# State products from rounded values and remainders, first weight tile ahead of x, and eight plans instead of four

## The chip, the cores and the metric

One core of one Trainium2 chip. The time is device microseconds of one execution. A profiled execution adds a trace of every instruction of the engines: PE (TensorE matmul), PEld (its weight loads), DVE (VectorE), ACT (ScalarE), POOL (GpSimd) and SP (SyncE, which here only issues DMAs).

## What is computed

Eight batches of 512 tokens `x` and 32 state rows `state`, eight heads of 64. Tokens read from the state and the state reads from the tokens, by softmax attention; both results go through a feed-forward layer with a squared ReLU.

```python
scale = 1.0 / np.sqrt(D)
a = softmax(scale * x @ state.T)         # per batch and head; 1e-9 in the denominator
xread = a @ state
a2 = softmax(scale * state @ x.T)
sread = a2 @ x
rows = concatenate([xread, sread])       # 8 * (512 + 32) = 4608 rows of 512
h = rows @ w_in                          # 512 x 2048
r = np.maximum(h, 0.0)
out = (r * r) @ w_out                    # 2048 x 512
```

The host only changes layouts, and hands `w_in` and `w_out` over as the two 32-bit words of float64 numbers, which the kernel turns into float32 itself.

## The kernel before, in words

**Algebra.** `xread` is never formed. Since `(a @ state) @ w_in = a @ (state @ w_in)`, the kernel makes `z = state @ w_in` for each head and uses it as the weight of the product with `a`.

**Two kinds of products.** A float32 matmul shows as two records in the trace. Most products are instead written as three matmuls on a rounded value (`hi`, type fp32r) and the remainder (`lo`): hi·hi, lo·hi, hi·lo. `split` (line 333) makes the two: a cast on ACT, then a subtraction on DVE or POOL.

**Units.** Work goes batch by batch (0 to 7) and within a batch over 16 blocks of 128 columns of `w_in` (`fc`); one (batch, block) pair is a unit. In a unit `up` (line 718) makes `h` in PSUM tile `ph` from `a_hi`, `a_lo` and `z_hi`, `z_lo` (six matmuls of 512 columns), then ReLU on ACT, the square on DVE or ACT, and the split into `g_hi` and `g_lo`. `down` (line 750) adds 12 matmuls of 512 columns into the four PSUM tiles `po`. After the last batch, 16 narrower units (256 columns) treat the state's rows.

**State products.** `z_part(G, k, g)` (line 401) makes `z` for four batches at a time (G 0: batches 0 to 3, G 1: batches 4 to 7), for a pair of blocks `k` and half of the heads `g`: 16 calls for each G. Each call has four float32 matmuls of 256 columns (line 410). Each of them uses 64 of the array's 128 rows; the two halves (`own`) alternate. Two ACT copies bring the result from PSUM to `z_stage`, and a DMA brings that to memory (`zd`). `z_fetch` (line 454) reads back what one batch needs, in four DMAs, and splits it. For the first six blocks of batch 0, `z_direct` (line 433) makes `z` without memory. The 16 calls for G 1 are put in when the code comes to batch 2.

**The start.** `w_tile(fc)` loads a 512 KB tile of `w_in` and `singles` (line 345) turns it into float32: an ACT step (line 352) and three DVE steps (lines 356, 361, 367). `wo_tile` does the same for `w_out` and splits the result. All of these tiles share four buffers with the tag `raw`. `scores(0, g)` loads `x` in two halves and makes the attention weights of batch 0, in a chain that goes between PE, ACT and DVE (`sq`, line 517, is its first product). `pad(0)` loads the state into the zeroed tile `sp_f`. Until there is something to do, PE works on up to 40 filler groups of four small matmuls (`keep_busy`, line 785, tile `idle`), at 0.4 us each in the plan.

**Who sets the order.** Every step is an `op` with an engine (or a choice of engines), a modelled cost, and the buffers that it reads and writes. `Planner.plan` (line 135) gives each op a due time, going back from the units' own due times (`plan.when`, line 328) by modelled costs and by `slack` times a scale. It then simulates the engines and takes, of the ops that can begin first, the one due first. A load counts its size / 330 + 2.2 us in the model. `Planner.run` (line 205) makes one plan for each of four scales, takes the one that ends first in the model, and issues the instructions in that order; on the chip each engine goes through its list in order and waits by semaphores.

Of the kernel before, what the change touches and what calls it, by code (L numbers as in the profile page):

```python
# [9 lines left out]
F32 = mybir.dt.float32  # L10
F32R = mybir.dt.float32r
# [33 lines left out]
class Planner:  # L45
# [1 line left out]

    RATE = 330.0
    NEAR = 1.0
    SLACKS = (1.5, 2.0, 2.5, 3.0)  # L50

    def __init__(self):
        self.ops, self.last_w, self.readers, self.chains = [], {}, {}, {}
        self.when = []

    def op(
        self, engs, run, r=(), w=(), lat=0.2, due=1e9, begin=0.0, size=0, both=False, hold=None,
# [147 lines left out]
    def run(self):  # L205

        plans = []
        for scale in self.SLACKS:
            log = self.plan(scale)
            plans.append((max(o.end for _, _, _, o in log), scale, log))  # L210
        log = min(plans)[2]
        for _, _, e, o in log:
            for k in o.bufs:
                if k.t is None:
                    k.t = k.make()
            o.run(e)
        return log
# [10 lines left out]
def dve(n):  # L228
    return ("DVE", 0.07 + n / 960)
# [6 lines left out]
def gps(n):  # L236
    return ("POOL", 0.15 + n / 450)
# [3 lines left out]
def memory_attention_then_relu2_ffn(  # L241
# [10 lines left out]
    nc = tc.nc  # L252
    P = 128
    B, C, S = xT.shape
    D = stT.shape[0]
    H = C // D
    N = stT.shape[1] // (H * B)
    DM, DF = w_out.shape[1] // 2, w_out.shape[0]
    R = S + N
    NG = H * N // P  # L260
    HG = H // NG
    NCC = DM // P
    NQ = NCC // NG
    NFC = DF // P
    NT = S // P
    FW = 256
    NFCH = DF // FW
    FPC = FW // P
    GB = P // N
# [9 lines left out]
    PLAIN_X = 2  # L279
    WARM = 40  # L280
    PARTS = [(b, 0, NFC) for b in range(B)]
    START, FIRST, STEP = 14.0, 4.9, 4.4

    const = ctx.enter_context(tc.tile_pool(name="const", bufs=1))
    sb = ctx.enter_context(tc.tile_pool(name="sb", bufs=2))
# [6 lines left out]
        raw=4, xraw=2, x_hl=1, z_stage=2, st_z=1, z_raw=2, z_hi=2, z_lo=2, a_hi=2, a_lo=2,  # L292
        sp_raw=2, st=2, at=1, st_low=1, q1=2, e2=4, s2=4, nm2=2, m1=2, s1=2, e_hl=1, both=1, low=1,
        r=2, g_hi=2, g_lo=2, os_=3, wof=2, po=4, ph=2, px=2,
    )

    plan = Planner()
    op = plan.op

    def tile_(shape, dtype, name, tag=None):  # L300
        tag = tag or name
        pool = {"po": ps_o, "ph": ps_h, "px": ps_x}.get(tag, sb)
        return Buf(pool, shape, dtype, name, tag, BUFS[tag], hot=tag in ("px", "x_hl"))
# [3 lines left out]
    sp_hl = const.tile([P, NG, 2, 2, 2 * N], F32R, name="sp_hl")  # L307
    sp_f = const.tile([P, NG, 2, P + D], F32, name="sp_f")
    nc.vector.memset(sp_f, 0.0)
    warm = const.tile([P, P], mybir.dt.bfloat16, name="warm")  # L310
    nc.vector.memset(warm, 0.0)
    nc.gpsimd.memset(sp_hl.bitcast(F32), 0.0)
    sr = [const.tile([P, C], F32, name=f"sr{i}") for i in range(NGB)]
    wi = const.tile([P, NFC, NCC, P], F32, name="wi")
    wo = [
# [8 lines left out]
    units = [(b, fc) for b, lo, hi in PARTS for fc in range(lo, hi)]  # L324
    begins = {}
    for u, (b, fc) in enumerate(units):
        begins.setdefault(b, u)
    plan.when = [START + FIRST * min(u, NFC) + STEP * max(0, u - NFC) for u in range(len(units))]
    plan.when += [plan.when[-1] + STEP + 2.8 * fc for fc in range(NFC + 1)]

    ENGINE = {"DVE": nc.vector, "POOL": nc.gpsimd, "SP": nc.sync, "ACT": nc.scalar}

    def split(hi, lo, src, n, r, wh, wl, engs=None, due=1e9, both=True, chain=None):

        op(
            act(n, 0.03 if both else 0.0), lambda e: nc.scalar.copy(out=hi(), in_=src()),  # L336
            r=r, w=wh, due=due, chain=chain,
        )
        op(
            engs or [dve(n)],  # L340
            lambda e: ENGINE[e].tensor_sub(out=lo(), in0=src(), in1=hi().bitcast(F32)),  # L341
            r=[*r, *wh], w=wl, due=due, both=both,
        )
# [29 lines left out]
    def load(out, in_, size, r=(), w=(), due=1e9, begin=0.0, hold=30.0, issue=0.42, eng="SP", chain=None, land=2.2):  # L373
        op(
            (eng, issue), lambda e: ENGINE[e].dma_start(out=out(), in_=in_()),
            r=r, w=w, size=size, due=due, begin=begin, hold=hold, chain=chain, land=land, slack=2.0,
        )


    def w_tile(fc):  # L380
        raw = tile_([P, NCC, P, 2], I32, "w_raw", "raw")
        load(lambda: raw.t.rearrange("p c f w -> p (c f w)"), lambda: w_in[fc], 512, w=[raw])
        singles(lambda: wi[:, fc], lambda: raw.t, [raw], [("wi", fc)])

    st = {}

    def z_state(G):
# [10 lines left out]
        half(1)  # L398
        st[G] = raw

    def z_part(G, k, g, begin=0.0):
        pz = [tile_([P, NQ, FW], F32, f"pz{i}", "px") for i in range(2)]
        stage = tile_([P, NQ, 2, FW], F32, "z_stage")

        def product(e):
            for q in range(NQ):
                for i in range(2):
                    own = slice(i * D, (i + 1) * D)
                    cc = g * NQ + q
                    nc.tensor.matmul(  # L410
                        pz[i].t[:, q, :], lhsT=st[G].t[own, cc, :], rhs=wi[own, k * FPC:(k + 1) * FPC, cc, :],
                        start=True, stop=True,
                    )

        op(("PE", 1.2), product, r=[("wi", k * FPC + i) for i in range(FPC)] + [(st[G], 0), (st[G], 1)], w=pz, begin=begin)
        for i in range(2):
            op(
                act(512), lambda e, i=i: nc.scalar.copy(out=stage.t[:, :, i, :], in_=pz[i].t),  # L418
                r=[pz[i]], w=[(stage, i)],
            )  # L420
        load(
            lambda: zd[G, k][:, g].rearrange("p h f -> p (h f)"),
            lambda: stage.t.rearrange("p q i f -> p (q i f)"), 512,
            r=[(stage, 0), (stage, 1)], w=[("zd", G, k, g)], eng="ACT", issue=0.35, hold=None, land=4.5,
        )
# [46 lines left out]
    def pad(b):  # L472
        pairs[b] = [tile_([P, NG, S], F32R, n) for n in ("a_hi", "a_lo")]
        src = stP[b].rearrange("p (g q n) -> p g q n", g=NG, q=2)
        rows = [slice(i * D, (i + 1) * D) for i in range(2)]
        at = [slice(i * N, (i + 1) * N) for i in range(2)]
        if b == 0:
            for i in range(2):
                load(
                    lambda i=i: sp_f[rows[i], :, :, at[i]], lambda i=i: src[rows[i]], 32,  # L480
                    w=[f"sp_f{i}"], issue=0.6, due=-4.0 - i,
                )
            return
        raw = tile_([P, NG, 2, N], F32, "sp_raw")
        load(lambda: raw.t, lambda: src, 64, w=[raw])
        for i in range(2):
            if b < PLAIN_X:
                op(
                    dve2(2 * N * NG), lambda e, i=i: nc.vector.tensor_copy(
                        out=sp_f[rows[i], :, :, at[i]], in_=raw.t[rows[i]]),  # L490
                    r=[raw], w=[f"sp_f{i}"],
                )
                continue
            split(
                lambda i=i: sp_hl[rows[i], :, :, 0, at[i]], lambda i=i: sp_hl[rows[i], :, :, 1, at[i]],
                lambda i=i: raw.t[rows[i]], 2 * N * NG, [raw], [("sp_hi", i)], [("sp_lo", i)],
            )
# [4 lines left out]
    def scores(b, g):  # L502
        xt = tile_([P, NQ, S], F32, "xt_raw", "xraw")
        load(
            lambda: xt.t, lambda: xT[b, g * CG:(g + 1) * CG, :].rearrange("(q p) s -> p q s", p=P),
            512, w=[xt], chain="x", due=1e9 if b else -10.0 + 8 * g,
        )
        q1 = tile_([P, NJ, N], F32, "q1")
        nm2 = tile_([P, 1], F32, "nm2")
# [15 lines left out]
        else:  # L525
            pst = tile_([P, S], F32, "st")
            for q in range(NQ):
# [8 lines left out]
                def product(e, hl=hl, pq=pq, q=q):  # L536
# [9 lines left out]
                    w=[pq],  # L546
# [292 lines left out]
    u = 0  # L839
    for b, lo, hi in PARTS:  # L840
        if b not in started:
            pad(b)
            for g in range(NG):
                scores(b, g)
            started.add(b)
        if lo == 0 and b >= 1:
            for g in range(NG):
                read(b - 1, g, At(begins[b] + 8), At(begins[b] - 1))
        if b == 2 and not z1[0]:
            z1[0] = True  # L850
            z_state(1)
            for m in range(NFC):
                z_part(1, *divmod(m, NG), begin=At(begins[2] + m * (begins[GB] - begins[2]) / (NFC + 4) - 1))
        po = [tile_([P, DM], F32, f"po{t}", "po") for t in range(NT)]
        for fc in range(lo, hi):
            k, i = divmod(fc, FPC)
            if (b, k) not in zs or (fc == lo and lo):
                z_fetch(b, k)
            f = slice(i * P, (i + 1) * P)

            z_hi, z_lo = zs[b, k]

            def todo(z_hi=z_hi, z_lo=z_lo, b=b, f=f):
                a_hi, a_lo = pairs[b]
                return [
                    (w.t[:, g, f], v.t[:, g, :])
                    for w, v in ((z_hi, a_hi), (z_lo, a_hi), (z_hi, a_lo))
                    for g in range(NG)
                ]

            r = [(z_hi, i), (z_lo, i)] + [(a, g) for a in pairs[b] for g in range(NG)]
            g_ = up(fc, S, todo, r, 3 * NG * pe(S)[1], u)
            down(po, fc, g_, fc == lo, fc == hi - 1, At(u + 2, -1.0))
            u += 1
        finish_part(b, lo, hi, po, At(u + 1))
    read(B - 1, 0, At(u - 6))
# [86 lines left out]
```

## Time and profile before

| | us |
|---|---|
| median of 3 runs | 699.78 (699.58 to 700.13) |
| the profiled execution's own time | 699.83 |
| its span in the trace | 698.0 |
| PE busy in the span | 687.4 |
| DVE busy | 364.4 |
| ACT busy | 424.0 |
| POOL busy | 143.4 |

The span goes from the first to the last instruction; the time of an execution has 1.83 us more. How to read the lines: `L763 PE MATMUL po<-wo_hi,g_hi` is line 763 of the kernel, on PE, which writes tile `po` from `wo_hi` and `g_hi`. In the chain that ended last, each row has its start, its length, and engine, tile and line; `x6` joins six instructions. `SPq` and `ACTq` are DMAs being issued from SP and from ACT. `[0.36 <-ACT r L733]` is the time that the engine stood idle before a row, and what ended that.

### The profile page before, as it was taken

The numbers are of one execution on the slowest core, as the hardware profiler recorded it, in microseconds if no ns is written. First come the engines' busy times: TensorE is split into PE (matmuls) and PEld (weight loads), VectorE is DVE, ScalarE is ACT, GpSimd is POOL, SyncE is SP. The second block draws the span as 40 slices with busy tenths as digits, with TensorE's granted clock in tenths as the row PEclk, the third lists the DMA queues.
The fourth block names the chain that finished last, engine by engine and source line by source line (L and its number), as shares of the span: only waits on it lengthen the run. The fifth ranks groups of instructions, "written<-read, shape, count | busy, mean of one in ns | idle before, by whom it ended". The sixth has DMA issues, their size and how long they took to land.

```text
span 698.0 us, 9735 instructions
## 1 busy us (share of the span) xinstructions
PE 687.4 (98%) x3352; PEld 549.9 (79%) x3352; DVE 364.4 (52%) x647; ACT 424.0 (61%) x801; POOL 143.4 (21%) x164
## 2 busy tenths in 40 slices
PE   8999999999999999999999999999999999999997
PEld 7766677888888888777787788888888888888896
DVE  4979996447537535731233366376467343333331
ACT  4667876657766557655565577566576555443553
POOL 0000000034524233310002144154423332000000
PEclk9999999999999999999999999999999999999999
DMA  6589982412231223243342332322232202100101
GB/s 230 193 329 316 312 272 79 167 60 92 65 121 62 60 80 102 85 160 125 128 158 77 109 106 60 121 90 66 62 121 74 78 24 87 32 10 1 61 1 31
DMA packets 49217, 76.92 MB, mean 110 GB/s; under 512 B 6800, under 2 KB 32528, under 8 KB 49168
## 3 DMA queue, kind: packets, MB, share of 16 engines
q1 hardware_dynamic: 44368, 59.27, 26.5%
q10 hardware_dynamic: 4800, 17.04, 6.1%
q8 instruction: 26, 0.43, 0.3%
q14 instruction: 23, 0.19, 0.1%
HBM read 50.59 MB, written 25.69 MB: 109 GB/s over the span
## 4 chain that ended last, share of the span: by engine, by line
PE 92%; DVE 3%; DMA 2%; ACT 1%; issue 1%; ACTq 0%; SPq 0%; DVEq 0%
PE po L763 53%; PE ph L727 28%; PE pz L410 4%; PE pr L668 2%; PE pq L538 2%; DMA w_raw<-w_in 1%; PE pt L650 1%; PE idle L790 1%; DMA wo_raw<-w_out 1%; PE sq L517 1%; DVE wi L361 0%; DVE wi L367 0%; ACT z_stage L418 0%; PE pzd L440 0%; DVE wof L367 0%
## 5 line engine op out<-in xcount | busy, mean ns | idle before, releaser
L763 PE MATMUL po<-wo_hi,g_hi 128*128 128x512 f32 x544 | 219.9, 404 | 0.1
L763 PE MATMUL po<-wo_lo,g_hi 128*128 128x512 f32 x544 | 215.5, 396 | 0.4 <-DVE wo_lo L341 0.4
L341 DVE TENSOR_TENSOR g_lo<-ph,g_hi 128x512 fp32r<-128x512 f32 (+1 forms) x144 | 94.5, 656 | 144.5 <-PE po L763 117.2
L763 PE MATMUL po<-wo_hi,g_lo 128*128 128x512 f32 x544 | 154.2, 395 | 0.0
L733 ACT ACTIVATE r<-ph 128x512 f32<-128x512 f32 (+1 forms) x144 | 82.8, 575 | 101.9 <-PE ph L727 101.8
L336 ACT CAST g_hi<-ph 128x512 fp32r<-128x512 f32 (+1 forms) x144 | 81.2, 564 | 91.3 <-PE po L763 88.3
L763 PEld LDWEIGHTS po<-wo_hi,g_hi 128*128 128x128 f32 x544 | 102.8, 189 | 28.6 <-issue 6.5
L763 PEld LDWEIGHTS po<-wo_lo,g_hi 128*128 128x128 f32 x544 | 102.9, 189 | 21.8 <-DVE wo_lo L341 0.7
L763 PEld LDWEIGHTS po<-wo_hi,g_lo 128*128 128x128 f32 x544 | 100.0, 188 | 23.5 <-issue 0.7
L741 DVE TENSOR_TENSOR ph<-ph,r 128x512 f32<-128x512 f32 (+1 forms) x65 | 44.6, 686 | 135.3 <-ACT r L733 134.9
L341 POOL TENSOR_TENSOR xn_hl<-xn_raw,xn_hl 128x512 fp32r<-128x512 f32 x32 | 43.6, 1361 | 286.2 <-ACT xn_hl L336 286.1
L727 PE MATMUL ph<-a_lo,z_hi 128*128 128x512 f32 x256 | 81.0, 397 | 0.0
L727 PE MATMUL ph<-a_hi,z_lo 128*128 128x512 f32 x256 | 80.7, 396 | 0.0
L727 PE MATMUL ph<-a_hi,z_hi 128*128 128x512 f32 x256 | 80.4, 395 | 0.0
L727 PEld LDWEIGHTS ph<-a_lo,z_hi 128*128 128x128 f32 x256 | 48.2, 188 | 11.8
L727 PEld LDWEIGHTS ph<-a_hi,z_hi 128*128 128x128 f32 x256 | 47.8, 188 | 12.2 <-issue 1.0
L727 PEld LDWEIGHTS ph<-a_hi,z_lo 128*128 128x128 f32 x256 | 48.1, 188 | 11.1
L341 DVE TENSOR_TENSOR z_lo<-z_raw,z_hi 128x512 fp32r<-128x512 f32 x61 | 47.0, 770 | 4.3 <-ACT z_hi L336 4.3
L341 POOL TENSOR_TENSOR xt_hl<-xt_raw,xt_hl 128x512 fp32r<-128x512 f32 x24 | 34.3, 1430 | 70.3 <-ACT xt_hl L336 70.3
L739 ACT ACTIVATE ph<-r 128x512 f32<-128x512 f32 (+1 forms) x79 | 44.8, 568 | 1.9
L418 ACT COPY z_stage<-pz 128x512 f32<-128x512 f32 x64 | 34.6, 589 | 14.6 <-PE pz L410 14.5
L410 PE MATMUL pz<-wi,st_z 64*128 64x256 f32 x256 | 37.5, 403 | 1.8 <-ACT z_stage L418 1.8
(122 smaller groups left out, 703.9 us busy)
## 6 DMA issues: line engine op xcount, KB each, us to landing
zd<-z_stage ACTq DMA_DIRECT2D x32, 512.0 KB, 3.2
z_raw<-zd SPq DMA_DIRECT2D x244, 64.0 KB, 2.3
xt_raw<-xT SPq DMA_DIRECT2D x16, 512.0 KB, 3.6
w_raw<-w_in SPq DMA_DIRECT2D x16, 512.0 KB, 5.7
wo_raw<-w_out SPq DMA_DIRECT2D x16, 512.0 KB, 5.9
xn_raw<-xn SPq DMA_DIRECT2D x16, 512.0 KB, 3.7
st_z<-stT SPq DMA_DIRECT2D x4, 128.0 KB, 5.4
sp_raw<-stP SPq DMA_DIRECT2D x7, 64.0 KB, 3.3
```

The source lines that it names most:

```text
L336: act(n, 0.03 if both else 0.0), lambda e: nc.scalar.copy(out=hi(), in_=src()),
L341: lambda e: ENGINE[e].tensor_sub(out=lo(), in0=src(), in1=hi().bitcast(F32)),
L410: nc.tensor.matmul(pz[i].t[:, q, :], lhsT=st[G].t[own, cc, :], rhs=wi[own, k * FPC:(k + 1) * FPC, cc, :], start=True, stop=True,)
L418: act(512), lambda e, i=i: nc.scalar.copy(out=stage.t[:, :, i, :], in_=pz[i].t),
L517: nc.tensor.matmul(sq.t, lhsT=sp_f[:, g].rearrange("p q n -> p (q n)")[:, q * P:(q + 1) * P], rhs=xt.t[:, q, :], start=q == 0, stop=q == N ...
L538: nc.tensor.matmul(pq.t, lhsT=sp_hl[:, g, q].rearrange("p i n -> p (i n)"), rhs=hl.t[:, i], start=i == 0, stop=i == 1,)
L668: nc.tensor.matmul(pr.t[:, q].rearrange("p i c -> p (i c)"), lhsT=eh.t[:, t, q].rearrange("p i n -> p (i n)"), rhs=hl.t[:, t].rearrange("p ...
L727: nc.tensor.matmul(ph.t[:, :width], lhsT=w, rhs=v, start=j == 0, stop=j == len(pairs_) - 1)
L733: act(width), lambda e: nc.scalar.activation(rl.t[:, :width], ph.t[:, :width], AF.Relu),
L739: nc.scalar.activation(ph.t[:, :width], rl.t[:, :width], AF.Square)
L741: nc.vector.tensor_mul(out=ph.t[:, :width], in0=ph.t[:, :width], in1=rl.t[:, :width])
L763: nc.tensor.matmul(po[t].t, lhsT=(g[0], g[0], g[1])[j].t[:, t * P:(t + 1) * P], rhs=wo[k][j % 2][:, i, :], start=first and j == 0, stop=la ...
```

## The change

1. `z_part(1, ...)`: the state's half (`z_halves`) and each pair of blocks of `w_in` (`w_halves`) are split into hi and lo, in buffers with the tag `raw`, and the four float32 matmuls become 12 of the hi/lo kind, of the same shapes. Both calls of a pair `k` may now begin at the same modelled time. For G 0 the float32 products stay. The modelled cost of a product is 0.85 for the new, 1.1 instead of 1.2 for the old.
2. The start: the loads of `sp_f` are due first, then `w_in`'s tile 0, then `x`; the first half of `x` is issued from ACT's queue, the second from SP's. The zeroing of `sp_hl` on POOL becomes an op that begins at 20 us in the plan.
3. The planner: slack scales 1.0 to 2.5 instead of 1.5 to 3.0, and two due-time tables (3.5 and 4.4 us for each of the first 16 units instead of 4.9), so eight plans instead of four. The due time of `down` goes from two units later less 1 us to one unit later plus 2 us.

```diff
-    SLACKS = (1.5, 2.0, 2.5, 3.0)
+    SLACKS = (1.0, 1.5, 2.0, 2.5)
...
-        for scale in self.SLACKS:
-            log = self.plan(scale)
-            plans.append((max(o.end for _, _, _, o in log), scale, log))
+        for when in self.whens:
+            for scale in self.SLACKS:
+                self.when = when
+                log = self.plan(scale)
+                plans.append((max(o.end for _, _, _, o in log), len(plans), log))
...
-    START, FIRST, STEP = 14.0, 4.9, 4.4
+    START, FIRST, STEP = 14.0, (3.5, 4.4), 4.4
...
-    nc.gpsimd.memset(sp_hl.bitcast(F32), 0.0)
+    op(("POOL", 0.6), lambda e: nc.gpsimd.memset(sp_hl.bitcast(F32), 0.0), w=[(n, i) for n in ("sp_hi", "sp_lo") for i in range(2)], begin=20.0)
...
-        load(lambda: raw.t.rearrange("p c f w -> p (c f w)"), lambda: w_in[fc], 512, w=[raw])
+        load(
+            lambda: raw.t.rearrange("p c f w -> p (c f w)"), lambda: w_in[fc], 512, w=[raw],
+            due=1e9 if fc else -50.0,
+        )
...
+    def z_halves():
+
+        raw = st[1]
+        hl = tile_([P, 2, NCC, GB * N], F32R, "st_hl", "raw")
+        split(
+            lambda: hl.t[:, 0], lambda: hl.t[:, 1], lambda: raw.t, NCC * GB * N,
+            [(raw, 0), (raw, 1)], [(hl, 0)], [(hl, 1)], engs=[gps(512)], chain="w1",
+        )
+        halves["st"] = hl
+
+    def w_halves(k, begin):
+        hi, lo = (tile_([P, FPC, NCC, P], F32R, n, "raw") for n in ("wz_hi", "wz_lo"))
+        for i in range(FPC):
+            split(
+                lambda i=i: hi.t[:, i], lambda i=i: lo.t[:, i], lambda i=i: wi[:, k * FPC + i], NCC * P,
+                [("wi", k * FPC + i)], [(hi, i)], [(lo, i)], engs=[dve(512), gps(512)], chain="w1", begin=begin,
+            )
+        halves[k] = hi, lo
...
+        def products(e):
+            s_hl = halves["st"]
+            for q in range(NQ):
+                cc = g * NQ + q
+                for j, (m, w) in enumerate(((0, 0), (1, 0), (0, 1))):
+                    for i in range(2):
+                        own = slice(i * D, (i + 1) * D)
+                        nc.tensor.matmul(
+                            pz[i].t[:, q, :], lhsT=s_hl.t[own, m, cc, :], rhs=w_hl[w].t[own, :, cc, :],
+                            start=j == 0, stop=j == 2,
+                        )
...
-                    w=[f"sp_f{i}"], issue=0.6, due=-4.0 - i,
+                    w=[f"sp_f{i}"], issue=0.6, due=-60.0,
...
-            512, w=[xt], chain="x", due=1e9 if b else -10.0 + 8 * g,
+            512, w=[xt], chain="x", due=1e9 if b else -12.0 + 4 * g, eng="SP" if b or g else "ACT",
...
-            for m in range(NFC):
-                z_part(1, *divmod(m, NG), begin=At(begins[2] + m * (begins[GB] - begins[2]) / (NFC + 4) - 1))
+            z_halves()
+            for k in range(NFCH):
+                at = begins[2] + k * (begins[GB] - begins[2]) / (NFCH + 2) - 1
+                w_halves(k, At(at - 1))
+                for g in range(NG):
+                    z_part(1, k, g, begin=At(at))
...
-            down(po, fc, g_, fc == lo, fc == hi - 1, At(u + 2, -1.0))
+            down(po, fc, g_, fc == lo, fc == hi - 1, At(u + 1, 2.0))
```

More of the change, by code (lines that the diff above doesn't have):

```diff
@@ L49 @@
     NEAR = 1.0
-    SLACKS = (1.5, 2.0, 2.5, 3.0)
+    SLACKS = (1.0, 1.5, 2.0, 2.5)
     def __init__(self):
         self.ops, self.last_w, self.readers, self.chains = [], {}, {}, {}
-        self.when = []
+        self.whens = []
     def op(
@@ L327, in memory_attention_then_relu2_ffn, with split @@
         begins.setdefault(b, u)
-    plan.when = [START + FIRST * min(u, NFC) + STEP * max(0, u - NFC) for u in range(len(units))]
-    plan.when += [plan.when[-1] + STEP + 2.8 * fc for fc in range(NFC + 1)]
+    plan.whens = []
+    for first in FIRST:
+        when = [START + first * min(u, NFC) + STEP * max(0, u - NFC) for u in range(len(units))]
+        plan.whens.append(when + [when[-1] + STEP + 2.8 * fc for fc in range(NFC + 1)])
     ENGINE = {"DVE": nc.vector, "POOL": nc.gpsimd, "SP": nc.sync, "ACT": nc.scalar}
-    def split(hi, lo, src, n, r, wh, wl, engs=None, due=1e9, both=True, chain=None):
+    def split(hi, lo, src, n, r, wh, wl, engs=None, due=1e9, both=True, chain=None, begin=0.0):
         op(
             act(n, 0.03 if both else 0.0), lambda e: nc.scalar.copy(out=hi(), in_=src()),
-            r=r, w=wh, due=due, chain=chain,
+            r=r, w=wh, due=due, chain=chain, begin=begin,
         )
@@ L399, in z_state @@
         st[G] = raw
+    halves = {}
+    def z_halves():
[14 more added lines that the diff above has]
+        halves[k] = hi, lo
     def z_part(G, k, g, begin=0.0):
@@ L403, in z_part @@
         stage = tile_([P, NQ, 2, FW], F32, "z_stage")
+        w_hl = halves.get(k) if G else None
         def product(e):
@@ L413, in product @@
                     )
-        op(("PE", 1.2), product, r=[("wi", k * FPC + i) for i in range(FPC)] + [(st[G], 0), (st[G], 1)], w=pz, begin=begin)
+        def products(e):
[9 more added lines that the diff above has]
+                        )
+        if G:
+            r = [(t, i) for t in (*w_hl, halves["st"]) for i in range(2)]
+            op(("PE", 0.85), products, r=r, w=pz, begin=begin)
+        else:
+            r = [("wi", k * FPC + i) for i in range(FPC)] + [(st[G], 0), (st[G], 1)]
+            op(("PE", 1.1), product, r=r, w=pz, begin=begin)
         for i in range(2):
```

## The prediction, made before the changed kernel ran

> **What bounds the kernel now.** I read the page first (busy time and the chain that ended last), then the busy time by stage, then the chain inside the stages that the change touches. From the page, the busy line and the two rows of the chain:
>
> ```profile
> span 698.0 us, 9735 instructions
> PE 687.4 (98%) x3352; PEld 549.9 (79%) x3352; DVE 364.4 (52%) x647; ACT 424.0 (61%) x801; POOL 143.4 (21%) x164
> PE 92%; DVE 3%; DMA 2%; ACT 1%; issue 1%; ACTq 0%; SPq 0%; DVEq 0%
> ```
>
> The busy time by stage (stage, its length, then busy us and count of PE, PEld, DVE, ACT and POOL, the granted clock, the DMA share and GB/s):
>
> ```profile
> 0.00:22.00 22.00, 18.75 (x173) 15.72 (x174) 12.62 (x27) 9.38 (x18) 1.17 (x7) 1.00 0.60 201
> 22.00:40.00 18.00, 16.11 (x95) 11.49 (x96) 16.19 (x31) 12.90 (x26) 0.00 (x0) 1.00 0.68 248
> 40.00:65.00 25.00, 24.14 (x124) 17.48 (x123) 21.42 (x42) 16.36 (x33) 0.00 (x0) 0.93 0.94 330
> 65.00:125.00 60.00, 60.00 (x283) 44.04 (x282) 51.65 (x95) 47.09 (x90) 2.52 (x2) 1.00 0.67 229
> 125.00:650.00 525.00, 524.89 (x2415) 422.46 (x2414) 247.77 (x427) 314.56 (x580) 139.73 (x155) 1.00 0.26 85
> ```
>
> From 65 us on PE never rests (60.00 of 60.00, 524.89 of 525.00), at full granted clock. A microsecond of matmul time removed there is a microsecond off the end, and so is each microsecond by which the start gets done sooner. Before 65 us it is different: PE has gaps of 3.25, 1.89 and 0.86 us, DVE is at 90% and 86% in the second and third rows, and DMA at 94% in the third. So there are two terms to price: the state products of batches 4 to 7, in the PE-bound stage, and the start, which PE does not bound.
>
> **The products, what one costs now.** In the chain, first an undisturbed unit (one block of w_in columns), then units with one of the old products, then a plain float32 product (sq) and the narrow products of the tail:
>
> ```profile
> 226.29 2.75 PE po L763 x12
> 229.05 1.41 PE ph L727 x6
> 230.46 2.75 PE po L763 x12
> ```
> ```profile
> 290.34 1.06 PE pz L410 x8
> 291.40 2.06 PE po L763 x8
> ...
> 295.79 1.06 PE pz L410 x8
> ```
> ```profile
> 94.86 1.72 PE sq L517 x4
> 96.58 1.84 PE po L763 x8
> ...
> 653.63 1.42 PE ph L727 x12
> ```
>
> A bare unit lasts 230.46 - 226.29 = 4.17 us, one with a product 295.79 - 290.34 = 5.45. So a product costs 1.28 us, not the 1.06 of its own row. The rest shows one row further: eight po matmuls take 2.06 behind it and 1.84 behind a product on all 128 rows.
>
> How much of the 1.28 is streaming? The source asks for four matmuls of 256 columns; the trace has eight records, two passes each. An sq record of 512 columns takes 1.72 / 4 = 0.43, so one of 256 takes 0.215. Eight in a row would be 1.72, more than the whole cost: the two halves of the array (rows 0 to 63 and 64 to 127) work side by side. The weight loads say the same:
>
> ```profile
> L410 PEld LDWEIGHTS pz<-wi,st_z x256: 182/186/187, 20.8 to 396.3; 64*128 64x128 f32 x128
> 295.72 0.73 PEld L410 LDWEIGHTS pz<-wi,st_z 64*128 64x128 f32 x8 [0.36 <-ACT r L733]
> 285.00:400.00 115.00, 18.15 (x128) 11.02 (x128) 17.17 (x32) 1.00 0.36 124
> ```
>
> Eight loads of 186 ns fit into 0.73. So streaming is 4 steps of pairs x 0.215 = 0.86, and 1.28 - 0.86 = 0.42 is lost in going from whole array to halves and back. It does not come with float32: sq is float32 on all rows, and its followers run at 1.84. The Trainium skill, TensorEngine Tiling (Array Packing), section Key Properties, says that a change of tiling mode drains the engine. The 0.42 agrees, and by that page it stays.
>
> **What one costs after.** Three single-pass products of high and low parts, 12 matmuls of 256 columns: 6 steps of pairs. The trace has no single-pass matmul on half the rows. The nearest row is the tail's ph, single-pass, 256 columns, a fresh 128-column weight each: 1.42 / 12 = 0.118. That gives 6 x 0.118 = 0.71, plus the 0.42 = 1.13. The saving is 1.28 - 1.13 = 0.15 a product. The last row above counts 128 records between 285 and 400 us, which is 16 products: 16 x 0.15 = **2.4 us**. Bounds: 16 x (1.28 - 0.71) = 9.1 gained if the 0.42 goes too; 16 x (12 x 0.118 + 0.42 - 1.28) = 9.0 lost if the pairs do not overlap. I take 2.4, because the rows show both the overlap and the loss to be matters of the half array.
>
> **The halves to be made.** 17 new casts on ACT and 17 subtractions on DVE or POOL. The nearest rows, and the landing of x:
>
> ```profile
> L336 ACT CAST xt_hl<-xt_raw x24: 603/620/622, 153.9 to 521.1; 128x512 fp32r<-128x512 f32 x24
> L341 POOL TENSOR_TENSOR xt_hl<-xt_raw,xt_hl x24: 1305/1313/1758, 154.6 to 521.8; 128x512 fp32r<-128x512 f32 x24
> ...
> DMA to landing us min/median/max: 3.4/3.6/9.3
> ```
>
> That is 17 x 0.62 = 10.5 us on ACT and at most 17 x 1.31 = 22.3 on POOL, while between 125 and 650 us ACT is idle for 525 - 315 = 210 and POOL for 385. I cost it at nothing; the cover is PE's own unbroken work. The buffers come from the weight loads' four, one held by the state, so the next pair of blocks waits for the last products. Were that chain bare, each of the eight pairs would put 0.62 + 1.31 = 1.9 on the path, 15 us in all.
>
> **The start.** The timeline (start, us, engine, what):
>
> ```profile
> 0.74 0.97 SPq L375 DMA_DIRECT2D xt_raw<-xT  x2
> 0.96 0.70 DVE L309 MEMSET sp_f<- 128x768 f32 x1 [0.96 <-PEq L953]
> 1.75 1.31 SPq L375 DMA_DIRECT2D sp_f<-stP  x2
> 1.79 6.29 PE L790 MATMUL idle<-warm 128*128 128x128 bf16 x60 [1.79 <-DVE warm L311]
> 3.11 1.07 SPq L375 DMA_DIRECT2D w_raw<-w_in  x2
> 7.08 0.66 ACT L352 ACTIVATE wi<-w_raw 128x512 f32<-128x512 f32 x1 [5.06 <-DMA w_raw<-w_in]
> 7.92 3.65 PE L517 MATMUL sq<-xt_raw,sp_f 128*128 128x512 f32 x8
> 10.51 0.69 DVE L621 TENSOR_REDUCE nm<-st 128x1 f32<-128x512 f32 x1 [2.31 <-ACT st L524]
> 11.12 0.68 DVE L361 SCALAR_TENSOR_TENSOR wi<-w_raw,wi 128x512 int32<-128x512 int32 x1
> 13.41 6.67 SPq L375 DMA_DIRECT2D w_raw<-w_in  x2
> 21.88 0.73 PE L727 MATMUL ph<-a_hi,z_hi 128*128 128x512 f32 x2
> ```
>
> The new first load on SP, sp_f, needs its memset, which ends at 1.66; so SP stands there, and behind it w_in's tile 0 and x's second half. Tile 0 is thus issued at about 3.1 as now, but with 512 KB of x less ahead of it. At the 330 GB/s of the third stage that is 1.6 us, so it is there at about 5.5 instead of 7.08. Its two long DVE steps (0.68 each) then lie in DVE's idle stretch before 9 us and no longer between the softmax steps. x's first half goes from ACT's queue. Its second half is issued 2.3 us later and lands at about 3.6 + 3.6 = 7.2, still ahead of its product at 7.92 + 1.8 = 9.7. By the planner's own constants what the first product needs, x's first half and sp_f, has landed at 0.42 + 576 / 330 + 2.2 = 4.4 instead of 0.42 + 1088 / 330 + 2.2 = 5.9 (the second half was ahead of sp_f), so some 11 fillers, one per 0.4, precede it instead of 15 (60 records / 4). At 6.29 / 15 = 0.42 each the product starts at 6.4: 1.5 us sooner.
>
> So DVE's chain to the first ph at 21.88 starts up to 1.5 sooner and is 1.4 shorter: between 1.4 and 2.9 us, and I take 2.2. It is passed on by two links:
>
> ```profile
> 28.63 8.13 DMA w_raw<-w_in
> ...
> 55.44 5.77 DMA wo_raw<-w_out
> ```
>
> Both are loads that waited for a buffer that DVE frees. Tile 0's buffer is free at about 8 instead of 13.4, ahead of stages with DMA shares of 0.60 and 0.68. So the **2.2 us** arrive at 65 us, and at the end. The new plan (due times of the first visit 1.4 or 0.5 us a unit tighter, less slack, best of eight by its own model) reorders the start as well. That cannot be read off; its bounds are 5 gained in all (DVE's buffer 5.4 sooner) and 3 lost (a landing of 8.13 where 5.77 was enough, with some of the work behind it).
>
> The remaining edits I cost at nothing: the memset put off on POOL (no POOL work between 22 and 65 us), and the earlier due time of the down products, which orders work on a PE that has no gap to fill.
>
> **Sum.** 698.0 - 2.4 - 2.2 = 693.4 of span; with the 699.83 - 698.0 = 1.83 outside it, **695.2 us**. The profiled execution's 699.83 stands 0.05 above the median of the runs, 699.78.
>
> **Rivals.**
> Slower: *the halves do not overlap in single-pass mode.* Today a pass streams for 0.215 and hides a load; a single pass of 0.118 may not. One matmul after the other gives +9.0 on the products and 699.8 + 9.0 - 2.2 = 706.6. It decides from a step of 0.86 / 6 = 0.143 on, where the products gain nothing. The eight loads in 0.73 speak against it. Chance 0.08.
> Slower still: *each load waits for the matmul on its own rows.* A step is then 0.186 + 0.118 = 0.30, a product 6 x 0.30 + 0.42 = 2.2, and the whole 699.8 + 16 x 0.94 - 2.2 = 712.6. In the old product this would have been 4 x (0.186 + 0.215) = 1.6 where 1.06 is seen. Chance 0.02. The Trainium skill, TensorE: Matmul & The Clock Gate, section Part 3, has this rule: loads overlap matmuls in flight only in other row groups. The 1.06 speaks against it.
> *The start's gain is swallowed*, since DMA is at 0.94 up to 65 us: 697.4. Chance 0.20.
> *The new order loses at the start* 3 us: 699.8 - 2.4 + 3 = 700.4; a plan with less slack has more such waits. Chance 0.12.
> *The 0.42 goes too*: 699.8 - 9.1 - 2.2 = 688.5. Chance 0.10.
> *The making of the halves is not covered*: up to 15 - 4.6 = 10 slower. Chance 0.03.
>
> **Numbers.** The forecast has the remaining 0.45, between 692.4 (start 5) and 698. The range 689 to 700.5 leaves out some 0.1 below and 0.1 above. A measurement tells 0.2% (1.4 us) from no change. Faster by more (under 698.4) are the forecast, the 0.42 going, and all but 0.05 of the swallowed start: 0.70. Within are that 0.05 and two thirds of the lost start: 0.13. Slower: 0.08 + 0.02 + 0.03 + 0.04 = 0.17.
>
> **What would show it.** A unit with a new product lasts 5.30 us, and po x8 behind it still takes 2.06; a gain of 0.5 a unit would refute the 0.42, and a unit over 5.45 the overlap. SP's first load stands until 1.7; the first ph comes near 19.7; PE's last gap ends near 62; no gap between 125 and 650. If the gap moves the other way, the reordering decided, and my start term is wrong.

## The result and the profile after

| | before | after |
|---|---|---|
| median us (range, runs) | 699.95 (699.58 to 700.70, 4) | 692.63 (690.83 to 693.09, 4) |
| ratio to before, 95% interval | | 0.9889 (0.9869 to 0.9910) |
| profiled execution: time, span | 699.83, 698.0 | 692.24, 690.5 |

The change makes the kernel 1.1% faster: 7.3 us between the medians, and 7.6 between the profiled executions (699.83 - 692.24), which the rest of this section takes apart. The ratio as recorded, 0.9889, would be 7.8 us of 700. The page of the changed kernel, the lines that answer to those of before:

```profile
span 690.5 us, 9927 instructions
PE 680.9 (99%) x3416; PEld 548.8 (79%) x3416; DVE 372.0 (54%) x652; ACT 431.9 (63%) x816; POOL 163.0 (24%) x178
PE 95%; DVE 2%; DMA 2%; ACT 1%; issue 0%; ACTq 0%
```

DVE, ACT and POOL carry more than before (the new halves), PE less, and it is still PE that the chain follows. By stage (columns as before):

```profile
0.00:22.00 22.00, 19.57 (x176) 15.74 (x177) 14.04 (x30) 11.89 (x22) 1.16 (x7) 1.00 0.85 272
22.00:40.00 18.00, 17.36 (x111) 13.13 (x110) 17.64 (x34) 13.95 (x28) 0.00 (x0) 1.00 0.92 321
40.00:65.00 25.00, 24.00 (x125) 17.36 (x125) 22.17 (x43) 18.38 (x35) 0.00 (x0) 1.00 0.93 304
65.00:125.00 60.00, 60.00 (x290) 45.13 (x287) 48.82 (x92) 45.83 (x88) 5.27 (x4) 1.00 0.61 212
125.00:650.00 525.00, 524.09 (x2501) 426.01 (x2500) 257.20 (x434) 323.04 (x599) 156.54 (x168) 1.00 0.26 84
```

Up to 40 us the DMA share went from 0.60 and 0.68 to 0.85 and 0.92, and DVE's work in the first 40 us from 28.8 to 31.7: the same work is done earlier. The granted clock is 1.00 in all five stages; before, it was 0.93 between 40 and 65.

The ph matmuls of unit 28 are a good mark for the start, as all state products for batches 0 to 3 lie ahead of them and none for batches 4 to 7 (the other matmuls ahead of them are the same number too, but for two filler groups). First the timeline's row for before, then for after:

```profile
174.06 0.62 PE L727 MATMUL ph<-a_hi,z_hi 128*128 128x512 f32 x2
```
```profile
167.43 0.62 PE L773 MATMUL ph<-a_hi,z_hi 128*128 128x512 f32 x2
```

So the **start** brought 174.06 - 167.43 = 6.6 us. The stages above account for part of it. PE's gaps up to 65 us went from 3.25 + 1.89 + 0.86 = 6.0 to 2.43 + 0.64 + 1.00 = 4.1, which is 1.9; the two filler groups fewer are some 0.6; and 25 us at a granted clock of 0.93 instead of 1.00 are at most 1.7 (the last section says why "at most"). The rest is not taken apart. The **products**, in the chain of the changed kernel:

```profile
288.21 0.91 PE pz L451 x9
289.12 2.05 PE po L809 x8
...
293.49 0.91 PE pz L451 x9
```

(The chain runs through nine of the twelve matmuls, because two run side by side; the trace has all twelve.) A unit with a product lasts 293.49 - 288.21 = 5.28 instead of 5.45: 16 x 0.17 = 2.7 us. po x8 behind it takes 2.05 as before, so the loss in changing to halves is still there. Two small things were **given back**. The timeline around 270 us and at the end:

```profile
269.60 0.35 ACTq L379 DMA_DIRECT2D zd<-z_stage  x1
269.62 0.36 SPq L379 DMA_DIRECT2D out<-os__2947  x1
...
275.36 0.58 ACT L825 COPY os__2995<-po 128x512 f32<-128x512 f32 x1 [4.05 <-DMA out<-os__2947]
276.00 0.50 PE L809 MATMUL po<-wo_hi,g_hi 128*128 128x512 f32 x1 [0.91 <-ACT os__2995 L825]
...
681.92 0.40 PE L836 MATMUL idle<-warm 128*128 128x128 bf16 x4
682.12 0.72 PE L809 MATMUL po<-wo_hi,g_lo 128*128 128x512 f32 x2
682.68 0.40 PE L836 MATMUL idle<-warm 128*128 128x128 bf16 x4
```

The first new product now ends where batch 2 ends. Its 512 KB to memory leave 0.02 us ahead of the batch's outputs; an output then lands after 5.64 us (before, most outputs of this size take 2.0 to 2.7, five take 3.9 to 4.3), its buffer is one of three, ACT waits for the buffer to write out the last po, and PE for that: 0.9 us. That the 512 KB hold the output up is read from the order of the issues; no run tests it. And the plan has put two filler groups that the start did not need into the tail: 0.6 us. Together 6.6 + 2.7 - 0.9 - 0.6 = 7.8, against 698.0 - 690.5 = 7.5 of span.

### The profile page after: what moved, and what is told of

Read it like the earlier page. It is cut to its first block, busy times and chain, and to the rows that moved or that the text cites. A ratio compares the mean times of both kernels' runs of the same rounds, so it can differ in the third digit from the quotient of the medians.

```text
span 690.5 us, 9927 instructions
## 1 busy us (share of the span) xinstructions
PE 680.9 (99%) x3416; PEld 548.8 (79%) x3416; DVE 372.0 (54%) x652; ACT 431.9 (63%) x816; POOL 163.0 (24%) x178
## 4 chain that ended last, share of the span: by engine, by line
PE 95%; DVE 2%; DMA 2%; ACT 1%; issue 0%; ACTq 0%
PE po L809 54%; PE ph L773 28%; PE pr L714 2%; PE pz L451 2%; PE pz L439 2%; PE pq L584 2%; PE idle L836 1%; PE pt L696 1%; PE sq L563 1%; DMA w_raw<-w_in 1%; DMA out<-os__2947 1%; PE pzd L486 0%; DVE wi L371 0%; PE pa L652 0%; ACT z_stage L464 0%
## 5 line engine op out<-in xcount | busy, mean ns | idle before, releaser
L340 ACT CAST z_hi<-z_raw 128x512 fp32r<-128x512 f32 x61 | 37.5, 615 | 0.3
```

## The experiments

All ratios are to the kernel before, run on the same chip; the changed kernel has 0.9889. One thousandth is 0.7 us. "Order" means the planner's order of instructions.

| run | ratio (95%) | us from before |
|---|---|---|
| the change | 0.9889 (0.9869 to 0.9910) | -7.8 |
| new order, old products | 0.9928 (0.9915 to 0.9941) | -5.0 |
| products alone | 0.9933 (0.9920 to 0.9946) | -4.7 |
| one modelled cost alone | 0.9972 (0.9956 to 0.9987) | -2.0 |
| start's loads alone | 0.9950 (0.9937 to 0.9964) | -3.5 |
| planner's part alone | 0.9973 (0.9961 to 0.9984) | -1.9 |
| change, first loads as before | 0.9889 (0.9873 to 0.9905) | -7.8 |
| change, table as before | 0.9951 (0.9938 to 0.9965) | -3.4 |
| change, batch 1's loads late | 0.9930 (0.9910 to 0.9950) | -4.9 |
| before, batch 1's loads early | 1.0060 (1.0047 to 1.0073) | +4.2 |
| change, measured costs in the plan | 0.9914 (0.9898 to 0.9930) | -6.0 |
| change, one half after the other | 0.9970 (0.9957 to 0.9982) | -2.1 |
| change, mode changed twice | 0.9972 (0.9956 to 0.9989) | -2.0 |

### What the products are worth

**New order, old products.** The rounded values and remainders are made and not read.

```diff
         def products(e):
+            return product(e)
             s_hl = halves["st"]
```

> The changed kernel with its own order of work, but the products for batches 4 to 7 are the four float32 matmuls again; the rounded values and remainders are still made and read by nobody. Theory (a product saves 5.45 - 5.28 = 0.17 us on a PE without gaps): 16 x 0.17 = 2.7 us slower than the changed kernel, near 695.3, a unit with a product 5.45. Rival (the whole gain is the start's, the products only changed places): as the changed kernel, 692.6. Rival (streaming alone counts, no loss in changing to halves): 9 slower, 701.7.

Measured 695.35 us, 0.0039 behind the change: 2.7 us. The chain's unit is 5.45 again:

```profile
289.83 1.06 PE pz L439 x8
...
295.28 1.06 PE pz L439 x8
```

That is the expected size, with every instruction's place the same; the products' saving is 16 x 0.17. The agreement of the medians to the tenth is luck (the six executions run from 694.56 to 696.36); the unit's length is the firmer evidence.

**One half of the array after the other.**

```diff
-            for q in range(NQ):
-                cc = g * NQ + q
-                for j, (m, w) in enumerate(((0, 0), (1, 0), (0, 1))):
-                    for i in range(2):
-                        own = slice(i * D, (i + 1) * D)
+            for i in range(2):
+                own = slice(i * D, (i + 1) * D)
+                for q in range(NQ):
+                    cc = g * NQ + q
+                    for j, (m, w) in enumerate(((0, 0), (1, 0), (0, 1))):
```

> The changed kernel, same order of work; inside a product the six matmuls of the array's upper half come first, then the six of the lower half, so that two matmuls side by side are always of the same half. Theory (the halves overlap only when they alternate; 0.118 us a step, 0.42 for the change of mode): a product goes from 1.11 to 12 x 0.118 + 0.42 = 1.84, 16 x 0.73 = 11.6 slower than the changed kernel, near 704.3. Rival (the queue reorders, or the halves never overlapped): as the changed kernel, 692.6. Rival (loads of a half wait for its own matmuls): over 0.30 a step, a product 4 us, 739.

Measured 698.18 us, 5.7 behind the change: half of what was expected. The chain of this run:

```profile
305.23 1.25 PE pz L451 x12
...
310.86 1.25 PE pz L451 x12
```

A unit lasts 5.63, a product 5.63 - 4.17 = 1.46. Without any overlap it would be 12 x 0.118 + 0.42 = 1.84, with full overlap 1.13. Nine steps give 9 x 0.118 + 0.42 = 1.48. The timeline of one product shows them:

```profile
305.16 0.50 PE L451 MATMUL pz<-wz_hi,st_hl 64*128 64x256 f32 x2
305.51 0.28 PE L451 MATMUL pz<-wz_lo,st_hl 64*128 64x256 f32 x1
305.51 0.51 PE L451 MATMUL pz<-wz_hi,st_hl 64*128 64x256 f32 x4
305.85 0.29 PE L451 MATMUL pz<-wz_lo,st_hl 64*128 64x256 f32 x2
305.98 0.39 PE L451 MATMUL pz<-wz_hi,st_hl 64*128 64x256 f32 x2
306.21 0.28 PE L451 MATMUL pz<-wz_lo,st_hl 64*128 64x256 f32 x1
```

The third matmul of each half is the first that reads `wz_lo`. The one at 305.51 belongs to the first half, and the `wz_hi` that begins beside it is the second half's first, though the source puts it seventh. The last three, from 305.98, run alone. So the overlap of the halves is real, losing half of it costs 5.7 us here, and the order in the source decides how much of it there is, though not as strictly as I had expected.

**The mode changed twice in a product.**

```diff
             for q in range(NQ):
                 cc = g * NQ + q
+                if q:
+                    nc.tensor.matmul(pz[0].t[:, q, :P], lhsT=warm, rhs=warm, start=True, stop=True)
```

> The changed kernel, same order of work; between the two groups of six matmuls of a product stands one small filler matmul on the whole array, whose result is overwritten. Theory (0.42 us for each time that the array goes to halves and back): 16 x (0.42 + 0.06) = 7.7 slower than the changed kernel, near 700.3. Rival (the 0.42 belongs to the first use of the PSUM tile or of the operands, not to the change of mode): 16 x 0.06 = 1 slower, 693.6.

Measured 698.24 us, 5.8 behind the change. In the chain a unit grows to 307.15 - 301.51 = 5.64:

```profile
301.51 0.55 PE pz L453 x6
...
307.15 0.55 PE pz L453 x6
```

That is 0.36 more than 5.28, of which the filler's own streaming is some 0.06. So one more trip from halves to the whole array and back costs 0.30 with such a small matmul in the middle, against 0.42 with large ones around. Less than 0.1 of the 0.30 may be the filler's own: in the tail of the changed kernel, without a change of mode, two groups of four fillers cost 0.6, which is 0.3 a group, against 4 x 0.06 of streaming. The rival (0.06 a product) is out: the loss belongs to the change of mode. It is what TensorEngine Tiling (Array Packing), Key Properties, in the Trainium skill says of mode changes, and these runs give it its price.

### What the start is worth, and what made it

**The products alone**, on the kernel before, with the new modelled costs (0.85, and 1.1 instead of 1.2), as in the first part of the diff.

```diff
+            z_halves()
+            for k in range(NFCH):
+                at = begins[2] + k * (begins[GB] - begins[2]) / (NFCH + 2) - 1
+                w_halves(k, At(at - 1))
+                for g in range(NG):
+                    z_part(1, k, g, begin=At(at))
```

> The kernel before with the new products alone (float32 replaced by 12 single-pass matmuls, the halves made, both calls of a pair beginning together); start, tables and slack as before. Theory: 699.95 - 2.7 = 697.2, up to 1 us more if the new order makes a wait like the one near 275 us of the changed kernel. Rival (the products bring nothing by themselves): 699.9.

Measured 695.83 us: 4.7 faster, 2.0 more than the products account for. In its trace unit 28 begins at 170.72 instead of 174.06, although this kernel changes nothing in the start. What does change there is the plan. (3.3 and 2.7 would be 6.0; a wait of PE for POOL of 1.4 us near 429 us, which the kernel before has not, takes part of it back.)

**One modelled cost alone.**

```diff
-        op(("PE", 1.2), product, r=[("wi", k * FPC + i) for i in range(FPC)] + [(st[G], 0), (st[G], 1)], w=pz, begin=begin)
+        op(("PE", 1.1), product, r=[("wi", k * FPC + i) for i in range(FPC)] + [(st[G], 0), (st[G], 1)], w=pz, begin=begin)
```

> The kernel before with one number changed: the planner's modelled cost of an old product 1.1 instead of 1.2, the value that the changed kernel has; no instruction is added, removed or altered, only ordered. Theory (each new plan orders the first 65 us anew, and this is where the products alone got more than their 2.7): 1 to 2 us faster than before, first ph of unit 28 near 171 instead of 174. Rival (the order at the start does not matter, the extra came from the products): 699.9.

Measured 698.33 us: 2.0 faster than before, with the same instructions in another order. 2.7 + 2.0 is the 4.7 of the run above, with intervals of about 1 us on each. (Its profiled execution, 695.58, was the fastest of its 12, so its trace is not used for sizes.)

**The start's loads alone.**

```diff
-                    w=[f"sp_f{i}"], issue=0.6, due=-4.0 - i,
+                    w=[f"sp_f{i}"], issue=0.6, due=-60.0,
...
-            512, w=[xt], chain="x", due=1e9 if b else -10.0 + 8 * g,
+            512, w=[xt], chain="x", due=1e9 if b else -12.0 + 4 * g, eng="SP" if b or g else "ACT",
```

(with tile 0's due time of -50 and the memset on POOL as an op)

> The kernel before with the start's loads alone: sp_f first, then tile 0 of w_in, x's first half from ACT's queue, sp_hl zeroed later. Theory of the prediction (tile 0 out of DVE's softmax stretch and its buffer free sooner): 2.2 us faster, 697.7, and the third w_in load after the first two issued near 8 to 10 us instead of 13.4. Rival (the tighter due times of the first visit made the start's gain): no change, 699.9.

Measured 696.92 us: 3.5 faster, more than the theory. Tile 0 can be begun at 7.02, no sooner than before to speak of, and the next w_in load after those at the very start goes out at 11.03 (8 to 10 expected, 13.41 before). But the first ph comes at 22.11, later than before (21.88), so it is not the earlier tile that brings it.

**The planner's part alone.**

```diff
-    SLACKS = (1.5, 2.0, 2.5, 3.0)
+    SLACKS = (1.0, 1.5, 2.0, 2.5)
...
-    START, FIRST, STEP = 14.0, 4.9, 4.4
+    START, FIRST, STEP = 14.0, (3.5, 4.4), 4.4
...
-            down(po, fc, g_, fc == lo, fc == hi - 1, At(u + 2, -1.0))
+            down(po, fc, g_, fc == lo, fc == hi - 1, At(u + 1, 2.0))
```

> The kernel before with the planner's part alone: slack scales 1.0 to 2.5, first-visit tables 3.5 and 4.4, the earlier due time of down. Theory (start's gain half from the loads, half from the order): 2.4 us faster, 697.5. Rival (the tables make all of the start's gain): 4.9 faster, 695.0. Rival (the loads make all of it): 699.9.

Measured 698.32 us: 1.9 faster. Products, loads and planner alone make 4.7 + 3.5 + 1.9 = 10.1, together 7.8: the parts do not add up. Each of them makes a new plan for the whole start, which would account for it.

**The change with the first loads as before**, the order of all else kept.

```diff
         log = min(plans)[2]
+        first = [next(x for x in log if x[3] is o) for o in self.first]
+        log = [("", "", "SP", x[3]) for x in first] + [x for x in log if x not in first]
...
+    loads = [o for o in plan.ops if o.size]
+    plan.first = [loads[i] for i in (2, 3, 0, 1, 4)]
```

> The changed kernel with its own order of work on all engines, but the first five loads in the old order on SP's queue (both halves of x, then sp_f, then tile 0 of w_in). Theory of the prediction (tile 0 early is what brings the start forward): about 2 slower than the changed kernel, 694.6. Rival (tile 0 landed at 7.1 in both kernels, so the position of these five loads is worth nothing by itself; it is the order that the planner made): as the changed kernel, 692.6, or a little faster as SP does not stand behind the memset.

Measured 691.92 us, ratio 0.9889, the same as the change. The rival holds: where these five loads stand is worth nothing by itself that could be told here (the intervals are 1.1 and 1.4 us to either side). The start of both, SP's timeline (and ACT's first step on tile 0) of the change, then SP's of this run:

```profile
1.69 1.32 SPq L379 DMA_DIRECT2D sp_f<-stP  x2
3.06 0.60 SPq L379 DMA_DIRECT2D w_raw<-w_in  x1
3.70 0.43 SPq L379 DMA_DIRECT2D xt_raw<-xT  x1
4.18 1.43 SPq L379 DMA_DIRECT2D w_raw<-w_in  x3
7.13 0.67 ACT L356 ACTIVATE wi<-w_raw 128x512 f32<-128x512 f32 x1 [4.64 <-DMA w_raw<-w_in]
...
15.09 1.16 SPq L379 DMA_DIRECT2D xt_raw<-xT  x2
```
```profile
0.74 0.97 SPq L382 DMA_DIRECT2D xt_raw<-xT  x2
1.75 1.31 SPq L382 DMA_DIRECT2D sp_f<-stP  x2
3.10 2.04 SPq L382 DMA_DIRECT2D w_raw<-w_in  x4
```

Tile 0 is issued at 3.1 in both, and ACT can begin on it at 7.13 in the change, at 7.08 in the kernel before. "Ahead of x" is there in the list, but not on the chip. What both have and the kernel before has not: four w_in tiles at once, and, as all else keeps its place, batch 1's x at 15 us instead of 41. These two do not make the gain by themselves either: the run of the planner's part alone, 1.9 us faster, has both of them:

```profile
3.09 2.03 SPq L379 DMA_DIRECT2D w_raw<-w_in  x4
...
13.34 1.73 SPq L379 DMA_DIRECT2D xt_raw<-xT  x2
```

**The change with the table as before** (one table, 4.9).

```diff
-    START, FIRST, STEP = 14.0, (3.5, 4.4), 4.4
+    START, FIRST, STEP = 14.0, (4.9,), 4.4
```

> The changed kernel with the first visit's due times at 4.9 us a unit as before (one table, four plans); products, first loads, slack scales and down's due time as changed. Theory (the tight table of 3.5 makes the order that got the start forward): the table's share of the start's 5 is lost, 3 slower than the changed kernel, near 695.5. Rival (any new plan gets about as much, the kernel before had an unlucky one): within 1.5 of the changed kernel, 692 to 694.

Measured 696.06 us: 4.3 behind the change. Take away the 2.7 of the products, and 0.7 is left of the start's gain. In the trace unit 28 begins at 171.95, 4.5 later than in the change. Given the rest of the change, it is the tight table that makes the good plan; on the kernel before, the planner's part alone brought only 1.9. Of its eight plans the changed kernel takes that of the table of 3.5 and the slack scale 1.5. The kernel before also takes 1.5, so the new scale of 1.0 has no part in it.

**Batch 1's loads late, in the change; early, in the kernel before.** Both keep the order on all else. `behind` is the load of one w_in tile, `fc` 9 in the first run and 3 in the second.

```diff
+        moved = [x for x in log if x[3] in self.moved]
+        log = [x for x in log if x[3] not in self.moved]
+        at = next(i for i, x in enumerate(log) if x[3] is self.behind) + 1
+        log[at:at] = moved
```

> The changed kernel with its own order of work, but the loads for batch 1 (two halves of x and the state, 1.1 MB) stand on SP's queue where the kernel before has them, behind the tenth tile of w_in, instead of behind the fifth at 15 us. Theory A (the start's gain is 1.1 MB moved out of the stage where DMA is full, 22 to 65 us, into the one where it is half idle): back by up to 1.1 MB / 330 GB/s = 3.3, near 695. Rival B (DMA volume in that stage is not what decides; the order on PE and DVE is): within 0.7 of the changed kernel, 692.3.

The tile behind which they stand was taken by its number, and the changed plan loads that tile as the eighth, so the loads went out at 26 us and not near 40. Measured 695.06 us, 2.9 behind the change, but spread from 691.88 to 696.49; the profiled execution is the fastest of these and shows no loss. The time agrees with theory A, without a trace that shows the place. The slower executions are those with a lower mean granted clock: 694.76 to 696.49 at 0.995 to 0.998, against 691.88 and 693.42 at 0.999 and 1.000. So a slow stretch of the clock may be part of the loss, whatever brings it about.

> The kernel before with its own order of work, but the loads for batch 1 stand behind the sixth tile of w_in, near 20 to 25 us, instead of near 41 us. Theory A (room in the DMA stage after 28 us is what the start lacks): up to 3.3 faster, 697. Rival B (the order on PE and DVE decides): 700. Rival C (the loads push back the tiles that PE waits for next): 1 to 3 slower, 702.

Measured 703.42 us: 4.2 slower, rival C. This run shows what the start hangs on. First, the kernel before: the chain up to PE's product at 39.69, and the stages around it; then the same stages and the chain of this run:

```profile
28.63 8.13 DMA w_raw<-w_in
...
36.78 0.67 ACT wi L352
...
39.15 0.49 ACT z_stage L418
...
39.69 1.61 PE pz L410 x8
```
```profile
35.00:40.00 5.00, 3.48 (x28) 2.29 (x27) 4.01 (x8) 2.83 (x6) 0.00 (x0) 1.00 0.75 295
40.00:45.00 5.00, 5.00 (x19) 3.77 (x18) 4.90 (x10) 2.83 (x6) 0.00 (x0) 0.68 0.90 292
```
```profile
35.00:40.00 5.00, 3.17 (x27) 1.99 (x25) 0.76 (x2) 1.51 (x3) 0.00 (x0) 1.00 1.02 415
40.00:45.00 5.00, 1.91 (x7) 1.72 (x8) 4.97 (x10) 3.50 (x7) 0.00 (x0) 0.66 0.49 167
45.00:50.00 5.00, 5.00 (x22) 3.75 (x20) 3.62 (x7) 1.75 (x4) 0.00 (x0) 0.66 0.99 318
```
```profile
27.92 10.55 DMA wo_raw<-w_out
...
38.49 0.66 ACT wof L357
...
42.46 0.59 ACT z_stage L425
```

Its waits of PE, the longest (total, count, longest in us):

```profile
PE pz L417 <- ACT z_stage L425: 4.8, 1, 4.8
```

ACT goes through its list in order. In it stands the first step on a weight tile that lands late, and some steps behind that the copy that frees a PSUM tile (z_stage), and for that PE waits. In both kernels the product that this copy brings out had ended at 30.9 and 30.8; the copy begins at 39.06 and 42.46. In the kernel before, the late tile on the chain is one of w_in, landing at 36.8 (L352); the gap on PE is 1.35 us, and the next 5 us have a mean granted clock of 0.68. In this run it is the w_out tile issued right behind the 1.1 MB, landing at 38.5 (L357; ACT is idle for 6.16 us before it); the gap is 4.75, and the clock 0.66 over 10 us. Early loads are no good in themselves; in the change, where they do no harm, the next tile seems not to be needed at once, which no run tests.

**The change with measured costs in the plan.**

```diff
-            op(("PE", 0.85), products, r=r, w=pz, begin=begin)
+            op(("PE", 1.11), products, r=r, w=pz, begin=begin)
...
-            op(("PE", 1.1), product, r=r, w=pz, begin=begin)
+            op(("PE", 1.28), product, r=r, w=pz, begin=begin)
```

> The changed kernel, and the planner reckons with what the products really cost on PE: 1.28 for an old one and 1.11 for a new one, instead of 1.1 and 0.85. Nothing but the order changes. Theory (a plan with truer costs stands nearer to what the chip does): 1 to 2 faster than the changed kernel, 691. Rival (the start is decided by landings that the model has too early, not by these costs): within 2 of the changed kernel on either side, 692.6.

Measured 693.26 us, 1.8 behind the change, with intervals that overlap. Truer costs of these products do not make a better order here; the rival holds.

## Why the prediction was right, point by point, and where it was not

The time lies in the range (689 to 700.5) and the direction is right, but 695.2 was 2.6 too high. The two terms did not fare alike, and that the sum came this near is in part luck: the early landing that the start term rests on did not come, a larger gain from the new order did, and 1.5 was given back that the sum had at nothing.

- **The products, 2.4: right in mechanism and size** (2.7, by trace and by the run with the old products). One costs 1.11 instead of the 1.13 expected, against 1.28. The 0.42 of the mode change stays (po x8 2.05), so the rival of 9.1 fell, and the runs above show both the overlap and the loss. The rule of the Trainium skill, TensorE: Matmul & The Clock Gate, Part 3, that loads overlap matmuls in flight only in other row groups, does not hold here: the new product loads a weight into each half at every step of 0.118 us, and such a load takes 0.185. The same section of the Trainium skill names a load into a background weight buffer as another case in which loads are pulled ahead; that would fit, and no run here shows it.
- **The halves at no cost: right for the making, wrong for what follows.** No product waited for them in the trace. But "no gap between 125 and 650" failed by 0.9 us: as far as the order of the issues shows, the result's way to memory met the outputs of batch 2. I had counted the new products' instructions on ACT, DVE and POOL and not where their DMA would now stand.
- **The start, 2.2: the step that failed.** "It is there at about 5.5 instead of 7.08": it was there at 7.13. SP standing until 1.69 and the first product at 6.64 came as forecast, but taking 512 KB of x from in front of the tile did not make it land sooner (7.08, 7.13, and 7.16 with the first loads as before), the first ph came at 21.23 and not 19.7, and the position of these loads is worth nothing (the run with the first loads as before). DVE's first long step on tile 0 did move, from 11.12 to 8.29, and its buffer came free at 10.58 instead of 13.41, but by the order: with the first loads as before the two are at 8.33 and 10.29. What came in its place is the reordering that the prediction bounded at 5 and did not price: 6.6 in the trace, 6.0 without the two filler groups that went to the tail. Given the rest of the change, the table of 3.5 us a unit makes most of it (4.3 are lost without it); on the kernel before, one modelled cost alone is worth 2.0. The prediction's own rows also had the granted clock at 0.93 from 40 to 65 us, and it gave that no price.
- **Rivals.** "The start's gain is swallowed" by a full DMA did not come; the gain came with a DMA share of 0.85 and 0.92 before 40 us, though no run shows that it came through it. A product of 1.11 also rules out two others: halves that do not overlap (0.56 above the old product) and loads that wait (0.94 above it).

What stays open is which of the moved steps in the start carry the 6.6. Shown are: not the first five loads; mostly the table, given the rest of the change; for the kernel before, one place where a late tile holds ACT's list. The late loads of batch 1 point to DMA room, or to the clock, as a part, but only in the timed runs.

## What to carry to other kernels

Price a replaced product by the spacing of whole units with and without it, not by its own row, and split that into streaming and the change of array mode; only the first shrank here with cheaper passes. Where a planner makes the order, any edit, even of one modelled cost, is also a new draw for every stage that the model gets wrong (here 2 us in 700), so measure a part with the order held, by changing what is issued after planning. On an engine that works in order, look for the short copy that stands behind a step waiting for a transfer: that copy, not the transfer's own user, was what PE waited for.

## What the runs showed of the hardware

- With the matmuls of one half of the array put ahead of the other's, a product took 1.46 us, between the 1.13 of full overlap and the 1.84 of none: part of the second half's work ran beside the first's. The second half's first matmul began 0.35 us after the first half's, beside its third, although six stand ahead of it in the source.
- The granted clock fell to a mean of 0.68 over 5 us after a gap of 1.35 us on PE (the kernel before), and of 0.66 over 10 us around one of 4.75 (batch 1's loads early). In the run of the planner's part alone a gap of 2.00 left it at 1.00, so the length of the gap alone does not decide. Whether the slow stretch costs the kernel before anything is not shown: nine of its executions had a mean granted clock of 0.998 or more, and took 698.93 to 702.07 us, against medians of 699.33 to 700.38 over all of them. The gap, and the two stages around it:

```profile
38.82 2.05 PE L444 MATMUL pzd<-wi,sp_f 128*128 128x128 f32 x16 [2.00 <-ACT z_stage L422]
```
```profile
35.00:40.00 5.00, 3.00 (x18) 2.33 (x18) 4.01 (x8) 1.62 (x3) 0.00 (x0) 1.00 0.95 340
40.00:45.00 5.00, 5.00 (x28) 3.59 (x27) 4.22 (x9) 4.08 (x9) 0.00 (x0) 1.00 0.81 306
```
